# One PSUM bank for the backward chain, a three-bank score ring, and a longer first segment in the backward weave of a mixed-attention kernel

## The chip, the cores and the metric

The kernel runs on one core of a Trainium2 chip. A core has a matrix engine (PE; its weight loads are listed as PEld), a vector engine (DVE), a scalar engine (ACT), GpSimd (POOL) and a queue engine that only issues transfers (SP). Matmuls write to PSUM, a memory of eight banks with 2 KB for each of 128 partitions; DVE and ACT read it from there. Sixteen DMA engines move data for all queues.

The metric is the device time of one launch in microseconds. The kernel before was run three times: 6249.93, 6255.53 and 6257.06 us, median 6255.53 us. The profile is of one more execution, of 6245.49 us, whose span from the first to the last instruction is 6243.7 us. Times of places in the trace are counted from the start of that span.

## The reference

The kernel computes a gated sum of two attention layers on 2048 tokens of width 576, and all gradients. Layer A is multi-query attention with 32 heads of width 18 and one shared key and value. Layer B is a recurrent layer with 32 heads of width 128: it works on 64 segments of 32 tokens, and 8 memory rows go from each segment to the next.

```python
def _A_ref(x, wq, wk, wv, wo):
    q = heads(x @ wq);  k = x @ wk;  v = x @ wv
    p = softmax(einsum('bhqd,bkd->bhqk', q, k) * Dh ** -0.5)
    return merge(einsum('bhqk,bkd->bhqd', p, v)) @ wo

def _B_ref(x, mem0, Wq, Wk, Wv, Wo, seg_len):
    mem = mem0
    for s in range(n_seg):
        h = concatenate([mem, x[:, s * seg_len:(s + 1) * seg_len]], axis=1)
        q, k, v = (einsum('btd,dhe->bhte', h, W) for W in (Wq, Wk, Wv))
        p = softmax(where(mask, einsum('bhqe,bhke->bhqk', q, k) * scale, -1e9))
        o = einsum('bhte,hed->btd', einsum('bhqk,bhke->bhqe', p, v), Wo)
        mem = o[:, :M]
        outs.append(o[:, M:])

out = g * A(x) + (1 - g) * B(x),  g = sigmoid((x * gate_w).sum(-1))
# returned: out and the gradients of all inputs for a given grad_out
```

So the backward pass of layer B is again a recurrence: the gradient of the memory rows goes from segment 63 down to segment 0.

## The kernel before

The program is a row of stages. The one that the change touches is the backward weave, from about 3118 to 4815 us. It puts two unrelated pieces of work together. The **chain** (`b_chain_bwd`) is the backward recurrence of layer B through the 64 segments. The **sweep** (`a_pass2`) is the second pass of layer A's backward attention, which recomputes the scores and gathers the gradients of the shared key and value.

Both are Python generators, and `weave` runs them in turn: one piece of the chain up to its `yield`, then `per_piece` steps of the sweep, which is 1 here. The order is written out by hand (`manual_schedule`), and each engine takes its instructions in the order in which the program issues them. What is left of the sweep runs after the chain.

**A step of the sweep**, n of 0 to 1024, handles two heads of one 128-row query block against 512 keys. It issues: `mm_S(n+1)`, the two score matmuls of the next step into `b_S` (a tile of two banks, one buffer); two matmuls into `b_dP` (one bank each, ring of three); `ex(n+1)`, the exponential of both score banks as one 1024-wide ACT instruction into `b_E`; two DVE multiplications `b_dS = b_dP * b_E` (L1585); and then the sums of step n-1: four matmuls of `b_dS` and `b_E` of that step into the accumulator `b_acc` (one bank). The score and `b_dP` matmuls use 32 rows of the array each, so the four can stand side by side; the four sums use 32 columns each and stand side by side too. Every four steps the SP queue loads one `b_QD` and one `b_SD`, two groups ahead.

**A segment of the chain** has 16 pieces:

- three pieces of `proj_part`: the gradient of the 8 memory rows times `WoT`, 40 matmuls of 512 columns into two banks (`r_pj` and `r_x`), each emptied by ACT into `r_dOm`;
- one of `mem_T` (8 small matmuls; ACT copies to `r_dOT`, DVE makes `r_prod`), one for `pd` (80 small matmuls; DVE makes `r_dS`, POOL spreads it out as `r_dSB`);
- `mem_grad` for three weights (16 small matmuls each into `r_x`, emptied by ACT into `r_dT`), the second and third of them with four `heads` units;
- the rest of the `heads` units, 48 in all: a unit is four matmuls of 288 columns side by side (`r_pj<-WT,r_dT`), 24 units fill one half of the sum, which ACT empties into `r_hs`;
- `sums` in two portions (fp32 matmuls into `r_x`), from which DVE writes the memory gradient `dm` for the next segment.

The eight banks of PSUM are all given out: `r_pj` 1, `r_x` 1, `b_S` 2, `b_dP` 3, `b_acc` 1. The weights `WT` (six transfers of 2304 KB) are loaded on the SP queue by `load_WT`, which the first segment (number 63) calls after its second piece; `WoT` is loaded before the stage, by SP and POOL.

Of the kernel before, what the change touches and what calls it, by code (L numbers as in the profile page):

```python
# [6 lines left out]
ACT = mybir.ActivationFunctionType  # L7
ALU = mybir.AluOpType
AX = mybir.AxisListType
BF16 = mybir.dt.bfloat16  # L10
F32 = mybir.dt.float32
P = 128

D = 576
NKT = 5
# [10 lines left out]
SCALEA = float(DA) ** -0.5  # L26
# [4 lines left out]
class Kern:  # L31
# [178 lines left out]

    def weave(self, chain, sweep, per_piece):
        with self.tc.manual_schedule():
            for _ in chain:
                for _ in range(per_piece):
                    next(sweep, None)
            for _ in sweep:
                pass
# [552 lines left out]
    def gate_load(self, tt, sp):  # L770
        r = slice(tt * P, (tt + 1) * P)
        L = []
        for nm, src, dt in (("o_b", self.b_dram, F32), ("o_go", self.grad_out, BF16)):
            t = sp.tile([P, D], dt, name=nm, bufs=1)
            self.nc.gpsimd.dma_start(t[:], src[r, :])
            L.append(t)
        t = sp.tile([P, NKT, P], BF16, name="o_T", bufs=1)
        self.nc.sync.dma_start_transpose(t[:], self.otok_dram[r, :])
        L.append(t)
        return L  # L780

    def gate(self, tt, L, wo, sp, psum):
        nc = self.nc
        bsb, go, oT = L
        diff = sp.tile([P, D], F32, name="o_diff", bufs=1)
# [23 lines left out]
    def load_WT(self):  # L809
        for wi in (2, 0, 1):  # L810
            for g in range(2):
                self.nc.sync.dma_start(self.WT[wi][:, 16 * g:16 * g + 16, :], self.st_WT[wi][:, 16 * g:16 * g + 16, :])

    def b_chain_bwd(self, keep, sp, psum):
        nc = self.nc
        NSEG = self.NSEG
# [37 lines left out]
        def p_blocks(pT):  # L854
            pq = to_q((pT[:, 1, :],), "p", nc.gpsimd)
            B = sp.tile([P, 8, 4, 8], BF16, name="r_PqB", bufs=1)
            self.expand(B[:], pq[:, 0, :, 0:8], 8)
            return B

        nxt = load(NSEG - 1)  # L860
        PqB = p_blocks(nxt["pT"])
        for s in reversed(range(NSEG)):
            L = nxt
            d_ = dm[s % 2]
            pT = L["pT"]
            nc.gpsimd.dma_start(self.dmT_dram[:, :, s, :], d_[:, :, 0:8])
            dOm = sp.tile([P, 8, E], BF16, name="r_dOm", bufs=1)
            pj = [psum.tile([P, 512], F32, name=nm, bufs=1) for nm in ("r_pj", "r_x")]
            for k, parts in enumerate((((0, (0, 1, 2, 3)),), ((0, (4,)), (1, (0, 1))), ((1, (2, 3, 4)),))):
                for j, kts in parts:  # L870
                    self.proj_part(pj[j], d_, self.WoT, j, kts)
                    if kts[-1] == 4:
                        self.evac(dOm[:, 4 * j:4 * j + 4, :].rearrange("p u e -> p (u e)"), pj[j][:], use="s")
                if s == NSEG - 1 and k == 1:
                    self.load_WT()
                yield
            src = self.mem_T(dOm, psum, "r_x", 1)
            dOT = sp.tile([P, 8, 4, 8], BF16, name="r_dOT", bufs=1)
# [28 lines left out]
            ph = {}  # L907
# [3 lines left out]
            def heads(n):  # L911
                for _ in range(n):
                    wi, hf, u = next(units)
                    if hf not in ph:
                        ph[hf] = psum.tile([P, 288], F32, name="r_pj", bufs=1)
                    for g in range(4):
                        self.mm(ph[hf][32 * g:32 * g + 32, :], lhsT=dT[:, wi, u, :],
                                rhs=self.WT[wi][:, 8 * g + u, 288 * hf:288 * hf + 288],
                                start=(wi == 2 and u == 0), stop=(wi == 1 and u == 7), tp=(0, 32 * g))
                    if wi == 1 and u == 7:  # L920
                        nc.scalar.copy(hs[:, 288 * hf:288 * hf + 288], ph[hf][:])

            def sums(kts):
                for kt in kts:
                    ncols = KT_ROWS[kt]
                    self.mm(pm[0:ncols, kt, :], lhsT=hs[:, kt * P:kt * P + ncols], rhs=self.selF[:, :])
# [13 lines left out]
            mem_grad(0, "r_x", ((rows(L["kx"]), blk(dSB)), (rows(mrow["k"]), blk(dSB, 8))))  # L940
            dSqB = sp.tile([P, 8, 4, 8], BF16, name="r_dSqB", bufs=1)
            self.expand(dSqB[:], dSq[:, 0, :, 0:8], 8)
            heads(4)
            yield
            heads(4)
            mem_grad(1, "r_x", ((rows(mrow["dx"]), [seln] * 8), (rows(mrow["q"]), blk(dSqB))))
            nc.gpsimd.dma_start(self.dTm_dram[s // 16][:, :, s % 16, :], dT[:].rearrange("p w u c -> p w (u c)"))
            if s:
                nxt = load(s - 1)
            yield  # L950
            heads(6)
            yield
            heads(6)
            xq = to_q((pT[:, 0, :], dS[:, 0, :]), "x", nc.gpsimd)
            for c in range(4):
                nc.gpsimd.dma_start(self.pq_dram[s // 4, s % 4, :, c, :, 32 * (s % 4):32 * (s % 4) + 32],
                                    xq[32 * c:32 * c + 8].rearrange("p i u k -> p (i u) k"))
            yield
            heads(4)
            yield  # L960
            heads(6)
            yield
            heads(6)
            pm = psum.tile([P, NKT, 8], F32, name="r_x", bufs=1)
            sums((0, 1))
            yield
            heads(6)
            if s:
# [1 line left out]
            yield  # L970
            heads(6)
            yield
            sums((2, 3, 4))
            dn = dm[1 - s % 2]
            nc.vector.tensor_copy(dn[:, 0:4, 0:8], pm[:, 0:4, :])
            nc.vector.tensor_copy(dn[0:64, 4, 0:8], pm[0:64, 4, :])
            yield
        pt = psum.tile([P, 8, P], BF16, name="r_x", bufs=1)
        for kt in range(NKT):
            rows = KT_ROWS[kt]  # L980
# [412 lines left out]
    def a_qd_end(self, p, qb, pq, absq, sp):  # L1393
        nc = self.nc
        self.mm(pq[0:64, :], lhsT=self.smneg[:, :], rhs=absq[:, :], start=False, stop=True, tp=(0, 0))
        QD = sp.tile([P, 512], BF16, name="a_QDs", bufs=3)
        nc.vector.tensor_copy(QD[:, :], pq[:, :])
        (nc.sync if qb % 2 == 0 else nc.gpsimd).dma_start(self.qd_dram[p][:, qb * 512:(qb + 1) * 512], QD[:, :])

# [131 lines left out]
    def a_pass2(self, keep, sp, psum):  # L1531
        nc = self.nc
        T, NTT = self.T, self.NTT
        KV = keep.tile([P, T], BF16, name="b_KV")
        nc.sync.dma_start(KV[:, :], self.kv_dram[:, :])
        Q, S, E_, D_ = {}, {}, {}, {}
        NC = 4 * NPR * NTT // 4

        def load(c):
            if c < NC:  # L1540
                p, q4 = (c // 4) % NPR, c % 4
                QD = sp.tile([P, 512], BF16, name="b_QD", bufs=3)
                nc.sync.dma_start(QD[:], self.qd_dram[p][:, q4 * 512:(q4 + 1) * 512])
                SD = sp.tile([P, 4, P], BF16, name="b_SD", bufs=3)
                nc.sync.dma_start(SD[:], self.sd_dram[p][:, 4 * q4:4 * q4 + 4, :])
                Q[c] = (QD, SD)

        def pair(n):
            return n // (NPR * NTT), n // 4, n % 4

        def mm_u(dst, n, base):
            kb, c, j = pair(n)
            for i in range(2):
                r = slice(base + 32 * i, base + 32 * i + 32)
                self.mm(dst[i], lhsT=Q[c][0][r, j * P:j * P + P], rhs=KV[r, kb * 512:kb * 512 + 512],
                        tp=(base + 32 * i, 0))

        def mm_S(n):
            S[n] = psum.tile([P, 2, 512], F32, name="b_S", bufs=1)
            mm_u([S[n][:, i, :] for i in range(2)], n, 0)  # L1560

        def ex(n):
            E_[n] = sp.tile([P, 2, 512], BF16, name="b_E", bufs=3)
            nc.scalar.activation(E_[n][:], S.pop(n)[:], ACT.Exp, scale=SCALEA)  # L1564

        load(0)
        load(1)
        mm_S(0)
        ex(0)
        acc = None  # L1570
        NS = NPR * NTT
        NP_ = 4 * NS
        for n in range(NP_ + 1):
            if n < NP_:
                if n % 4 == 2:
                    load(n // 4 + 2)
                if n + 1 < NP_:
                    mm_S(n + 1)
                dP = [psum.tile([P, 512], F32, name="b_dP", bufs=3) for _ in range(2)]
                mm_u([t[:] for t in dP], n, 64)  # L1580
                if n + 1 < NP_:
                    ex(n + 1)
                D_[n] = sp.tile([P, 2, 512], BF16, name="b_dS", bufs=2)
                for i in range(2):
                    nc.vector.tensor_tensor(out=D_[n][:, i, :], in0=dP[i][:], in1=E_[n][:, i, :], op=ALU.mult)  # L1585
            if n > 0:
                o = n - 1
                if o % NS == 0:
                    acc = psum.tile([P, 512], F32, name="b_acc", bufs=1)
                SD = Q[o // 4][1]  # L1590
                src = (D_.pop(o), E_.pop(o))
                for i4 in range(4):
                    self.mm(acc[32 * i4:32 * i4 + 32, :], lhsT=SD[:, o % 4, 32 * i4:32 * i4 + 32],
                            rhs=src[i4 // 2][:, i4 % 2, :],
                            start=(o % NS == 0), stop=(o % NS == NS - 1), tp=(0, 32 * i4))
                if o % NS == NS - 1:
                    dkv = sp.tile([P, 512], BF16, name="b_dkv", bufs=1)
                    nc.scalar.copy(dkv[:], acc[:])
                    k0 = (o // NS) * 512
                    nc.sync.dma_start(self.dkv_dram[:, k0:k0 + 512], dkv[:])  # L1600
            yield
# [229 lines left out]
```

The softmax here doesn't subtract the row's maximum and nothing guards it: scores larger than these inputs give would overflow.

## Time and profile before

| | us | remark |
|---|---|---|
| median of three runs | 6255.5 | 6249.9 to 6257.1 |
| span of the profiled run | 6243.7 | granted PE clock 0.974 in the mean |
| backward weave | 3118 to about 4815 | loads up to 3144, last sums just after 4811 |
| its steady part, segments 62 to 0 | 3196 to 4807 | PE busy 1484.9, DVE 1403.6, ACT 1207.6, POOL 577.3 of 1611 us |
| its first part | 3118 to 3196 | DMA busy nearly all of it up to 3181 |

In a group line the parts are: line, engine, operation, what is written and read, the shape, the count, then busy time and mean nanoseconds of one, then the idle time of the engine just ahead of these instructions and what ended it. Matmuls that stand side by side overlap, so a group's busy time is less than count times mean. All matmuls have line 66 because a helper records them; they are told apart by the tiles that they write and read. Consecutive instructions of ACT or DVE overlap a little in their records, since the next one starts while the last one is still writing.

### The profile page before, as it was taken

To read this page: it belongs to the slowest core of one execution; us is meant where nothing else is said; L and a number is where in the kernel's file an instruction comes from. 1 tells how busy PE (TensorE), PEld (TensorE's weight loads), DVE (VectorE), ACT (ScalarE), POOL (GpSimd) and SP (SyncE) were. 2 spreads that over 40 slices of the span, in tenths; PEclk is the share of its full clock that TensorE was granted. 3 is DMA by queue.
4 is the path that set the end of the run, shared out by engine and by line. 5 is a ranking of instruction groups with operands and counts; after the bars stand their busy time and mean duration, and the time that the engine had idled before them with its cause. 6 is when DMAs were issued, how large, how long until landed. Compare 5 with 4: busy or idle time off the path is not lost.

```text
span 6243.7 us, 208736 instructions
## 1 busy us (share of the span) xinstructions
PE 5691.9 (91%) x88611; PEld 3321.0 (53%) x88822; DVE 3743.0 (60%) x7061; ACT 3500.1 (56%) x5105; POOL 1952.9 (31%) x3451
## 2 busy tenths in 40 slices
PE   7898999999999985999869999999998999899996
PEld 5443444444444434777735555555554777674443
DVE  4336777777777773666558888888887111121111
ACT  3326787778777873656557777777776222111101
POOL 3002343434343342444423333333333111122213
PEclk9999999999999997999989999999999999999998
DMA  4646666666675536999864444444444999996643
GB/s 153 223 151 120 126 125 127 126 127 125 127 125 107 105 85 181 249 257 258 245 207 107 109 109 108 108 111 109 110 108 103 244 244 250 243 261 196 222 150 114
DMA packets 1368111, 991.97 MB, mean 159 GB/s; under 512 B 931613, under 2 KB 1184806, under 8 KB 1356486
## 3 DMA queue, kind: packets, MB, share of 16 engines
q1 hardware_dynamic: 1285030, 780.53, 52.1%
q0 software_dynamic: 82144, 198.05, 10.0%
q8 instruction: 696, 11.40, 0.8%
q14 instruction: 241, 1.97, 0.1%
HBM read 552.41 MB, written 384.76 MB: 150 GB/s over the span
## 4 chain that ended last, share of the span: by engine, by line
PE 64%; ACT 15%; issue 9%; DMA 6%; SPq 3%; POOL 2%; DVE 1%; ACTq 0%; POOLq 0%; DVEq 0%
ACT b_E L1564 10%; PE w_acc L66 10%; PE a_acc L66 8%; PE c_x L66 6%; PE b_S L66 6%; PE a_S L66 5%; PE c_pj L66 5%; PE p_pb L66 4%; PE r_pj L66 4%; ACT a_E L1422 3%; PE r_x L66 2%; DMA dsx_dram<-x_dS 2%; PE x_tr L71 2%; PE b_acc L66 2%; PE x_po L66 1%
## 5 line engine op out<-in xcount | busy, mean ns | idle before, releaser
L1455 DVE TENSOR_TENSOR a_W<-a_dP,a_E 128x512 bf16<-128x512 f32 x2048 | 1316.2, 685 | 413.2 <-PE a_dP L66 289.7
L1585 DVE TENSOR_TENSOR b_dS<-b_dP,b_E 128x512 bf16<-128x512 f32 x2048 | 1312.9, 683 | 241.8 <-issue 119.6
L1564 ACT ACTIVATE b_E<-b_S 128x1024 bf16<-128x1024 f32 x1024 | 1048.9, 1024 | 446.3 <-PE b_dP L66 322.0
L1422 ACT ACTIVATE a_E<-a_S 128x1024 bf16<-128x1024 f32 x1024 | 1050.6, 1026 | 218.5 <-PE a_dP L66 182.9
L66 PE MATMUL b_S<-b_KV,b_QD 32*128 32x512 bf16 x2048 | 401.1, 382 | 155.2 <-ACT b_E L1564 100.7
L66 PE MATMUL r_pj<-WT,r_dT 128*32 128x288 bf16 x12288 | 493.5, 287 | 1.5 <-issue 1.5
L66 PE MATMUL w_acc<-w_d,w_h 128*128 128x512 bf16 (+1 forms) x2352 | 471.0, 379 | 2.5
L66 PE MATMUL a_acc<-a_E,l_VK 128*32 128x512 bf16 x4096 | 401.6, 380 | 27.9 <-ACT a_acs L1460 27.8
L66 PE MATMUL a_S<-a_QD,l_KV 32*128 32x512 bf16 x2048 | 398.5, 384 | 24.7 <-ACT a_E L1422 15.3
L66 PE MATMUL b_acc<-b_dS,b_SD 128*32 128x512 bf16 x2048 | 419.3, 391 | 0.6 <-DVE b_dS L1585 0.2
L66 PE MATMUL a_acc<-a_W,l_WK 128*32 128x512 bf16 x4096 | 411.8, 390 | 0.2 <-DVE a_W L1455 0.2
L66 PE MATMUL b_acc<-b_E,b_SD 128*32 128x512 bf16 x2048 | 404.0, 391 | 0.0
L66 PE MATMUL b_dP<-b_KV,b_QD 32*128 32x512 bf16 x2048 | 401.2, 386 | 0.0
L66 PE MATMUL a_dP<-a_QD,l_KV 32*128 32x512 bf16 x2048 | 398.1, 385 | 0.0
L66 PEld LDWEIGHTS <-r_dT 128*32 128x32 bf16 x12288 | 333.2, 97 | 80.5 <-issue 2.6
L1055 DVE COPY y_T<-y_pt 128x512 bf16<-128x512 bf16 x256 | 97.1, 420 | 461.5 <-PE y_pt L71 461.4
L66 PEld LDWEIGHTS <-b_QD 32*128 32x128 bf16 x4096 | 164.9, 91 | 345.7 <-issue 284.7
L66 PEld LDWEIGHTS <-w_h 128*128 128x128 bf16 (+1 forms) x2400 | 213.0, 100 | 244.6 <-issue 3.4
L66 PEld LDWEIGHTS <-hm 128*32 128x32 bf16 x7680 | 188.2, 96 | 186.4 <-issue 14.6
L1041 ACT CAST y_tdk<-y_pk 128x512 bf16<-128x512 f32 x128 | 75.1, 587 | 377.0 <-PE y_pk L66 212.5
L66 PEld LDWEIGHTS <-l_KV 32*128 32x128 bf16 x4096 | 118.9, 91 | 297.4 <-issue 275.3
L66 PE MATMUL y_pdx<-WT,y_T 128*128 128x288 bf16 x2048 | 272.8, 287 | 0.0
(416 smaller groups left out, 11401.9 us busy)
## 6 DMA issues: line engine op xcount, KB each, us to landing
b_QD<-qd_dram SPq DMA_DIRECT2D x256, 128.0 KB
b_SD<-sd_dram SPq DMA_DIRECT2D x256, 128.0 KB
dOx_dram<-p_tok SPq DMA_DIRECT2D x16, 1024.0 KB
c_vx<-vx_dram SPq DMA_DIRECT2D x256, 64.0 KB
krow_dram<-c_k POOLq DMA_DIRECT2D x64, 256.0 KB, 3.0
qrow_dram<-c_q POOLq DMA_DIRECT2D x64, 256.0 KB, 3.4
vrow_dram<-c_v POOLq DMA_DIRECT2D x64, 256.0 KB, 3.0
x_q<-qx_dram SPq DMA_DIRECT2D x32, 512.0 KB
```

Of the source, the lines that this page charges most:

```text
L66: return self.nc.tensor.matmul(out, lhsT, rhs, start=start, stop=stop, tile_position=tp, skip_group_check=True)
L71: return self.nc.tensor.transpose(out, in_, self.identB[b:b + nrows, b:b + nrows], tile_position=tp)
L1041: nc.scalar.copy(d[w][:, r, :], pk[:])
L1055: nc.vector.tensor_copy(T_[t][w][:], pt[:])
L1422: nc.scalar.activation(E_[n][:], S.pop(n)[:], ACT.Exp, scale=SCALEA)
L1455: nc.vector.tensor_tensor(out=W_[n][:, i, :], in0=dP[i][:], in1=E_[n][:, i, :], op=ALU.mult)
L1564: nc.scalar.activation(E_[n][:], S.pop(n)[:], ACT.Exp, scale=SCALEA)
L1585: nc.vector.tensor_tensor(out=D_[n][:, i, :], in0=dP[i][:], in1=E_[n][:, i, :], op=ALU.mult)
```

## The change

All of it lies in the backward weave.

- **Weave.** A piece may now yield a number; then so many sweep steps follow it (a plain `yield` still means one).
- **Chain on one bank.** `r_pj` is gone; the projection, the `heads` sums and everything else use `r_x`. The projection has two pieces of 20 matmuls instead of three. The third `mem_grad` and the second one stand alone, all `heads` come after them in eight pieces of six units, and `sums` is one piece at the end. There are 16 pieces still; the last yields `s % 2`, so in even segments no sweep step stands between `sums` and the next segment's projection.
- **First segment.** `load_WT` moves ahead of the loop and to the POOL queue, behind a one-column copy `r_seen` that reads the last block of `WoT`. Then 11 sweep steps follow ahead of the first projection, 4 after the third `mem_grad`, and 10 after each of the first two `heads` pieces.
- **Sweep.** `b_S` is a ring of three one-bank tiles (two for each step), so the exponential is two 512-wide instructions. The sums of step n-2, not n-1, are issued in step n; `b_E` has four buffers and `b_dS` three. `b_dkv` shares the ring of `b_QD`.

```diff
-            for _ in chain:
-                for _ in range(per_piece):
+            for steps in chain:
+                for _ in range(per_piece if steps is None else steps):
...
-                self.nc.sync.dma_start(self.WT[wi][:, 16 * g:16 * g + 16, :], self.st_WT[wi][:, 16 * g:16 * g + 16, :])
+                self.nc.gpsimd.dma_start(self.WT[wi][:, 16 * g:16 * g + 16, :], self.st_WT[wi][:, 16 * g:16 * g + 16, :])
...
+        seen = sp.tile([P, 1], BF16, name="r_seen", bufs=1)
+        nc.gpsimd.tensor_copy(seen[:], self.WoT[:, NKT - 1, 0:1])
+        self.load_WT()
+        yield 11
         for s in reversed(range(NSEG)):
+            first = s == NSEG - 1
...
-            pj = [psum.tile([P, 512], F32, name=nm, bufs=1) for nm in ("r_pj", "r_x")]
-            for k, parts in enumerate((((0, (0, 1, 2, 3)),), ((0, (4,)), (1, (0, 1))), ((1, (2, 3, 4)),))):
-                for j, kts in parts:
-                    self.proj_part(pj[j], d_, self.WoT, j, kts)
-                    if kts[-1] == 4:
-                        self.evac(dOm[:, 4 * j:4 * j + 4, :].rearrange("p u e -> p (u e)"), pj[j][:], use="s")
-                if s == NSEG - 1 and k == 1:
-                    self.load_WT()
+            for j in range(2):
+                pj = self.proj_mem(d_, self.WoT, j, psum, "r_x", 1)
+                self.evac(dOm[:, 4 * j:4 * j + 4, :].rearrange("p u e -> p (u e)"), pj[:], use="s")
                 yield
...
-                        ph[hf] = psum.tile([P, 288], F32, name="r_pj", bufs=1)
+                        ph[hf] = psum.tile([P, 288], F32, name="r_x", bufs=1)
...
-            heads(4)
-            yield
-            heads(4)
+            yield
             mem_grad(1, "r_x", ((rows(mrow["dx"]), [seln] * 8), (rows(mrow["q"]), blk(dSqB))))
...
-            yield
+            yield 4 if first else 1
             heads(6)
-            yield
+            yield 10 if first else 1
+            heads(6)
+            yield 10 if first else 1
             heads(6)
...
-            pm = psum.tile([P, NKT, 8], F32, name="r_x", bufs=1)
-            sums((0, 1))
...
-            sums((2, 3, 4))
+            pm = psum.tile([P, NKT, 8], F32, name="r_x", bufs=1)
+            sums(range(NKT))
...
-            yield
+            yield s % 2
...
-            S[n] = psum.tile([P, 2, 512], F32, name="b_S", bufs=1)
-            mm_u([S[n][:, i, :] for i in range(2)], n, 0)
+            S[n] = [psum.tile([P, 512], F32, name="b_S", bufs=3) for _ in range(2)]
+            mm_u([t[:] for t in S[n]], n, 0)
...
-            E_[n] = sp.tile([P, 2, 512], BF16, name="b_E", bufs=3)
-            nc.scalar.activation(E_[n][:], S.pop(n)[:], ACT.Exp, scale=SCALEA)
+            E_[n] = sp.tile([P, 2, 512], BF16, name="b_E", bufs=4)
+            for i, t in enumerate(S.pop(n)):
+                nc.scalar.activation(E_[n][:, i, :], t[:], ACT.Exp, scale=SCALEA)
...
-        for n in range(NP_ + 1):
+        for n in range(NP_ + 2):
...
-                D_[n] = sp.tile([P, 2, 512], BF16, name="b_dS", bufs=2)
+                D_[n] = sp.tile([P, 2, 512], BF16, name="b_dS", bufs=3)
...
-            if n > 0:
-                o = n - 1
+            if n > 1:
+                o = n - 2
...
-                    dkv = sp.tile([P, 512], BF16, name="b_dkv", bufs=1)
+                    dkv = sp.tile([P, 512], BF16, name="b_dkv", tag="b_QD", bufs=3)
```

More of the change, by code (lines that the diff above doesn't have):

```diff
@@ L958, in b_chain_bwd @@
             yield
-            heads(4)
+            heads(6)
             yield
@@ L1541, in load @@
                 p, q4 = (c // 4) % NPR, c % 4
-                QD = sp.tile([P, 512], BF16, name="b_QD", bufs=3)
+                QD = sp.tile([P, 512], BF16, name="b_QD", tag="b_QD", bufs=3)
                 nc.sync.dma_start(QD[:], self.qd_dram[p][:, q4 * 512:(q4 + 1) * 512])
```

## The prediction

> **What bounds the kernel now.** I read the page first for the place of the stage, then the chain of waits inside one segment, then the timelines of PE and DVE there, and last the stretches at its start.
>
> The chain of waits, from 3954 us on (start, length, what):
>
> ```profile
> 3961.01 1.03 ACT b_E L1564
> 3962.08 0.39 PE b_S L66 x2
> 3962.47 0.08 PE b_dP L66 x2
> 3962.56 1.03 ACT b_E L1564
> 3963.63 0.39 PE b_S L66 x2
> 3964.11 1.03 ACT b_E L1564
> 3965.18 0.39 PE b_S L66 x2
> ```
>
> A closed circle: the scores need the bank that the exponential reads, the exponential needs the scores. 3962.08 to 3963.63 to 3965.18 is 1.55 us each time. That is the floor of a step while PE, DVE and ACT each have less to do.
>
> The PE timeline shows where a step is longer:
>
> ```profile
> 3958.59 0.39 PE L66 MATMUL b_S<-b_KV,b_QD 32*128 32x512 bf16 x2
> 3958.92 0.39 PE L66 MATMUL b_acc<-b_dS,b_SD 128*32 128x512 bf16 x2
> ...
> 3959.14 0.91 PE L66 MATMUL r_pj<-WT,r_dT 128*32 128x288 bf16 x24
> 3959.99 0.61 PE L66 MATMUL r_x<-selF,r_hs 128*128 128x8 f32 x4
> 3960.53 0.39 PE L66 MATMUL b_S<-b_KV,b_QD 32*128 32x512 bf16 x2
> ...
> 3974.82 0.39 PE L66 MATMUL b_acc<-b_dS,b_SD 128*32 128x512 bf16 x2
> ...
> 3975.15 0.19 PE L66 MATMUL r_x<-r_dSB,r_kx 128*128 128x32 bf16 x1
> ...
> 3975.65 0.67 PE L66 MATMUL r_pj<-WT,r_dT 128*32 128x288 bf16 x16
> 3976.25 0.39 PE L66 MATMUL b_S<-b_KV,b_QD 32*128 32x512 bf16 x2
> ```
>
> From start to start: scores and dP 0.33, sums 0.22, six heads units 0.85, two of the five portions of `sums` 0.54; a `mem_grad` 0.50 after 0.33 for the sums and the change of tile shape. One segment is 12 steps at 1.55, and 1.94 (heads with `sums`), 1.76 and 1.65 (`mem_grad` with heads) and 1.61 (a step behind `r_xq` on DVE): 25.56 us. The `dmT_dram` transfers of two segments start at 3196.46 and 3222.01, 25.55 us apart. 63 segments: 3196 to 4807, 25.57 us each.
>
> DVE, same place, and then the stretches (length, busy PE, PEld, DVE, ACT, POOL, clock, DMA share, GB/s):
>
> ```profile
> 3956.23 2.56 DVE L1585 TENSOR_TENSOR b_dS<-b_dP,b_E 128x512 bf16<-128x512 f32 x4
> ...
> 3961.05 1.29 DVE L1585 TENSOR_TENSOR b_dS<-b_dP,b_E 128x512 bf16<-128x512 f32 x2 [0.65 <-issue]
> ```
>
> ```profile
> 3144.00:3162.00 18.00, 14.09 (x239) 5.78 (x239) 9.84 (x18) 10.05 (x14) 3.83 (x6) 0.69 1.02 422
> 3162.00:3181.00 19.00, 0.26 (x4) 0.11 (x4) 0.00 (x0) 0.36 (x1) 1.20 (x3) 0.50 1.06 407
> ...
> 3196.00:4807.00 1611.00, 1484.87 (x31327) 833.59 (x31323) 1403.63 (x2511) 1207.63 (x1510) 577.30 (x1006) 1.00 0.43 108
> ```
>
> Four `b_dS` of 0.68 in 2.56 give a pitch of (2.56 - 0.68) / 3 = 0.627, so 1.25 us of DVE a step. DVE is busy 22.3 us a segment (1403.6 / 63), PE 23.6. The circle hides how near they are. From 3162 to 3181 nothing computes: a `b_QD` stands behind `WT` in the SP queue.
>
> **What the Trainium skill says.** PSUM — Partial Sum Buffer, PSUM bank collisions: engines must not touch one bank and quadrant at once, so writers wait for readers by bank. The trace agrees: scores restart 0.05 after the exponential ends. ScalarE: Activation LUTs, What ACT_TABLE_LOAD costs: an activation takes 186 ns + 0.833 ns an element, and neighbours overlap by 93 ns. The trace has 1024 ns for 1024 (1039 by the page) and 579 to 588 for the 512-wide copies of `r_dOm`. TensorEngine Tiling (Array Packing), Key Properties: changing the tiling mode drains the array; the 0.33 above against 0.22 agrees. DMA: Bandwidth & Descriptors, Queues, rings and completion order: an engine goes round its queues packet by packet. No run here shows how that falls out between `WT` and the sweep's loads.
>
> **The change part by part**, against the profiled span, which stands 12 us under the median.
>
> *Score ring.* The circle goes: the next step's second score matmul needs only the first half of the exponential, about 0.48 + 0.6 after the step's start, so 1.13. Two 512-wide exponentials cost ACT 2 x 0.5 for 0.92, +0.1 a step, beside PE (by the page's price 2 x 0.52). ACT then has some 15.5 x 1.0 + 3 in a segment of over 24. The next floor is DVE: the second `b_dP` of a step takes the bank of the first `b_dS` of the last step, which starts 0.52 after the scores and lasts 0.68: 1.20 at best, 1.25 when DVE is never idle.
>
> *Sums two steps late.* Same matmuls; the wait of PE for `b_dS` (0.2 in the 1.61 step) goes. Buffers are SBUF only. One more iteration is under 1 us. `b_dkv` in the `b_QD` ring delays one load at four places; the loads run two groups ahead: nothing.
>
> *A segment now*, step with piece:
> - Projection, two pieces: 0.55 + 1.19 each. (12 and 16 matmuls show 0.82 and 1.04, so 20 give 1.26, and the next scores start about 0.07 before that end.) The second waits for its bank: ACT empties the first 0.59 after its end, PE is back after 0.55 less a tail: +0.15. Sum 3.63.
> - `mem_T`, `pd`, three `mem_grad`: PE has 0.98 + 1.50 + 3 x 1.19 = 6.1, but DVE 5 x 1.25 + `r_prod` 0.22 + `r_dS` 0.22 + `r_dspad` and `r_dsq` 0.58 (start to start in the DVE timeline) = 7.3, and it waits in order for `r_dOT`, 0.1: 7.4.
> - Eight pieces of six heads: 8 x (0.33 + 0.22 + 0.84) = 11.1; `r_xq` (0.63) overruns by 0.3, `r_pq` and two handovers of the bank 0.1: 11.5.
> - `sums`: 0.55 + 0.11 + 10 x 0.13 = 1.96. In even segments the step is gone, but PE waits about 0.5 for `dm` (3965.11 to 3965.65 before): no gain.
>
> Together 24.5, against 25.57: 1.07 less, x 63 = -67 us. It has 15.5 steps, not 16; the other half steps are paid at the start.
>
> *First segment.* It now holds 48 sweep steps: 24.5 + 32.5 x 1.25 + 3 for the clock of 0.69 = 68 us from the first scores, for 52 (3144.5 to 3196.3): +17 if no load is late. `WT` on POOL frees the SP queue of 4.0 us of issues, but its 14 MB still take 39 us (3141.6 to 3180.7). If its 18 KB rows alternate with the 1 KB rows of `b_QD` and `b_SD`, the sweep gets only 8 to 12 steps in by 3180 and ends the segment near 3231: +35. `r_seen` waits for `WoT`, but PE and `r_ppad` ahead of it wait as long (3136, 3137.4); behind it stand `WT` and the chain's stores, which nobody needs soon. I take +26.
>
> Net -67 + 26 = -41: 6255.5 - 41 = **6214 us** (span about 6203).
>
> **The rivals.**
> 1. *One bank turns into the circle* (slower). Eight handovers of `r_x` a segment, each a copy of 0.37 to 0.59 plus whatever exponential half ACT is in. Before, two banks and 1.55 us steps hid this. For it: ACT is in order, and in the 1.25 us steps it still holds exponentials at the next piece. Against: a step's 0.55 to 0.66 of PE stands between pieces. At 0.2 us more each: 26.1 a segment, +33 + 26: 6314. It decides from 25.2 on, 0.09 us a handover.
> 2. *PE and DVE overlap better* than stretch by stretch. The sums above without the waits and with 15.5 steps give PE 22.3 in all, DVE 15.5 x 1.25 + 2.4 = 21.8. At 23.5: 63 x 2.07 = -130, +22: 6147. For it: rings one step deeper. Against: the `b_dP` ring is still three.
> 3. *A wash*: `WT` starves the sweep (+35) and small waits bring 25.0: -36 + 35: 6255. The change then doesn't fill the gap as it says.
>
> **How the numbers follow.** Forecast 0.52, its own range 6189 to 6243 (24.2 to 24.9 a segment, start +20 to +30); rival 2 0.18; rival 3 0.12; rival 1 0.18. About 0.2% (12.5 us) can be told from no change: faster 0.52 + 0.18, same 0.12, slower 0.18. The range leaves out the fastest end of rival 2 (about 0.07) and the larger part of rival 1 (about 0.12): 6158 to 6288.
>
> **What would show it.** Score matmuls that no longer wait for `b_E`; `dmT_dram` transfers about 49 us apart for two segments; heads steps of 1.39; DVE without gaps from `mem_T` to the third `mem_grad`; PE idle before `dOm` and `r_x` under 0.2. The start is judged by when segment 62 begins (3213 to 3231) and by waits for `b_QD`. I am wrong in the main step if the segments come 25.2 us apart or more, or if PE waits for ACT at most handovers.

## The result, and the profile after

| | before | after |
|---|---|---|
| median of six runs each, us | 6254.82 (6248.08 to 6262.6) | 6217.08 (6210.39 to 6222.2) |
| span of the profiled run, us | 6243.7 | 6215.3 |
| first segment: issue of the `WoT` loads to the start of segment 62, us | 76.4 (3120.03 to 3196.46) | 119.2 (3123.86 to 3243.09) |
| mean from start to start of segments 62 to 0 (62 intervals), us | 25.68 | 24.34 |

The ratio is 0.994 (95% interval 0.9927 to 0.9953): 37.7 us less by the medians, where 41 less was forecast. The two parts of the forecast sum are each further off than that. The 62 intervals between segment starts bring 62 x (24.34 - 25.68) = -83 us, and the first segment takes +42.8. Together that is -40 for the stage. A mark behind the stage says the same: its first transfer of `h_hist` starts 35.9 us earlier than before (4832.03 for 4867.92), although the stage began 3.8 us later in this profile, so 39.7 were gained in it. The two spans differ by only 28.4, because this execution of after took 3.8 us more ahead of the stage and 7.5 us more behind that mark.

Segment starts are read from the POOL timeline, where one `dmT_dram` transfer leaves for each segment. Columns: start, length, engine, line, operation, count, and in brackets the idle time ahead and what ended it. First the kernel after:

```profile
3123.86 1.18 POOL L516 DMA_DIRECT2D WoT<-st_WoT  x2 [11.95 <-DMA dqx_dram<-x_dq]
...
3243.09 0.89 POOL L871 DMA_DIRECT2D dmT_dram<-dm  x1 [2.34 <-DVE dm L975]
3267.32 0.90 POOL L871 DMA_DIRECT2D dmT_dram<-dm  x1 [2.35 <-DVE dm L975]
3291.42 0.89 POOL L871 DMA_DIRECT2D dmT_dram<-dm  x1 [2.34 <-DVE dm L975]
...
4752.28 0.90 POOL L871 DMA_DIRECT2D dmT_dram<-dm  x1 [2.34 <-DVE dm L975]
```

The same view of the kernel before, its last segment:

```profile
4788.46 0.90 POOL L866 DMA_DIRECT2D dmT_dram<-dm  x1 [2.73 <-DVE dm L976]
```

(4752.28 - 3243.09) / 62 is 24.34; most intervals are 24.23 and 24.10 in turn, so two segments take 48.3, as the forecast asked for (about 49). The starts of before, 3196.46 to 4788.46, give 1592.0 / 62 = 25.68. The forecast had used 25.57, from 1611 us over 63 segments; most intervals of before are 25.57, but every few segments one takes 0.3 to 1.0 more.

The PE timeline of after inside one segment, the score and `b_dP` matmuls and one piece of heads:

```profile
3980.09 0.39 PE L66 MATMUL b_S<-b_KV,b_QD 32*128 32x512 bf16 x2
...
3980.70 0.37 PE L66 MATMUL b_dP<-b_KV,b_QD 32*128 32x512 bf16 x1 [0.22 <-DVE b_dS L1585]
...
3981.83 0.39 PE L66 MATMUL b_S<-b_KV,b_QD 32*128 32x512 bf16 x2
...
3982.42 0.91 PE L66 MATMUL r_x<-WT,r_dT 128*32 128x288 bf16 x24
3983.26 0.39 PE L66 MATMUL b_S<-b_KV,b_QD 32*128 32x512 bf16 x2
...
3984.66 0.39 PE L66 MATMUL b_S<-b_KV,b_QD 32*128 32x512 bf16 x2
...
3986.05 0.39 PE L66 MATMUL b_S<-b_KV,b_QD 32*128 32x512 bf16 x2
...
3993.97 1.27 PE L66 MATMUL r_x<-selF,r_hs 128*128 128x8 f32 x10
...
3995.59 1.26 PE L66 MATMUL r_x<-WoT,dm 128*32 128x512 bf16 x20 [0.35 <-DVE dm L975]
3996.78 0.39 PE L66 MATMUL b_S<-b_KV,b_QD 32*128 32x512 bf16 x2
```

PE's waits above 0.15 us in after, from 3250 to 4700 (what waited and what released it; us in all, times, longest); two more are of 0.2 us each:

```profile
PE b_dP L66 <- DVE b_dS L1585: 13.4, 60, 0.3
PE r_x L66 <- DVE dm L975: 10.4, 30, 0.3
PE b_S L66 <- DMA b_QD<-qd_dram: 5.7, 8, 2.2
```

No score is among these with a wait for the exponential. A step with heads takes 3984.66 - 3983.26 = 1.40 and then 1.39. The `mem_grad` step from 3980.09 to 3981.83 is longer, 1.74, and what ends the wait in it is DVE: the second `b_dP` matmul of the step waits for a bank that `b_dS` still reads. The last three lines of the timeline are an even segment, with no step between `sums` and the projection: PE is idle for 0.35 until DVE has written `dm`.

The DVE timeline at the same place:

```profile
3973.11 1.29 DVE L1585 TENSOR_TENSOR b_dS<-b_dP,b_E 128x512 bf16<-128x512 f32 x2 [0.43 <-issue]
3975.43 1.29 DVE L1585 TENSOR_TENSOR b_dS<-b_dP,b_E 128x512 bf16<-128x512 f32 x2 [1.03 <-ACT r_dOm L63]
...
3980.00 6.51 DVE L1585 TENSOR_TENSOR b_dS<-b_dP,b_E 128x512 bf16<-128x512 f32 x10
```

DVE has gaps around the projection (0.43 and 1.03 here) and none from `mem_T` to the third `mem_grad`: PE sets the pace in one stretch, DVE in the other.

In the groups of after (line, engine, operation, what is written and read, shape, count, busy time and mean ns, idle time ahead and its releaser) the single biggest wait of the score matmuls is now a transfer:

```profile
L1564 ACT ACTIVATE b_E<-b_S 128x512 bf16<-128x512 f32 x2048 | 1114.7, 599 | 253.9 <-PE b_dP L66 210.6
...
L66 PE MATMUL b_S<-b_KV,b_QD 32*128 32x512 bf16 x2048 | 417.7, 389 | 57.9 <-DMA b_QD<-qd_dram 57.3
```

51.5 of those 57.3 us (41.78, 5.26 and 4.43) are in the first segment. (The 41.78 count from the end of PE's work in the stage before; 23.4 of them pass ahead of the issue of `WT`. Before has 26.6 us of waits for `b_QD` there and 18.4 for `WoT`.) The PE timeline of this segment and the stretches there (length, busy PE, PEld, DVE, ACT, POOL, clock, DMA share, GB/s), both of after:

```profile
3161.61 1.01 PE L66 MATMUL b_S<-b_KV,b_QD 32*128 32x512 bf16 x3 [41.78 <-DMA b_QD<-qd_dram]
...
3173.32 0.60 PE L66 MATMUL b_S<-b_KV,b_QD 32*128 32x512 bf16 x2 [5.26 <-DMA b_QD<-qd_dram]
...
3184.61 0.61 PE L66 MATMUL b_S<-b_KV,b_QD 32*128 32x512 bf16 x2 [4.43 <-DMA b_QD<-qd_dram]
```

```profile
3144.00:3162.00 18.00, 0.39 (x3) 0.16 (x4) 0.00 (x0) 0.00 (x0) 3.30 (x6) 0.50 1.02 388
3162.00:3190.00 28.00, 15.15 (x86) 2.98 (x86) 13.27 (x22) 12.56 (x24) 0.00 (x0) 0.50 0.83 338
```

The DMA engines are full from 3144 to 3162 and PE, DVE and ACT do nothing: the first scores come 18.4 us after `WT` began to be issued (3143.22), and the scores of only eight steps are begun before 3184.61. The 32 extra steps (11, 3, 9 and 9 above one step a piece) were to fill the time in which `WT` arrives, and for much of that time their own inputs are not there. Before has begun just as many, eight, when its wait for `b_QD` ends at 3180.74: the gap holds no more steps than it did.

### The profile page after: what moved, and what is told of

Same layout as the page of the kernel before. It is cut to its first block, busy times and chain, and to the rows that moved or that the text cites. A ratio compares the mean times of both kernels' runs of the same rounds, so it can differ in the third digit from the quotient of the medians.

```text
span 6215.3 us, 210597 instructions
## 1 busy us (share of the span) xinstructions
PE 5734.9 (92%) x88611; PEld 3278.1 (53%) x88822; DVE 3724.6 (60%) x7061; ACT 3545.8 (57%) x6129; POOL 1950.7 (31%) x3458
## 5 line engine op out<-in xcount | busy, mean ns | idle before, releaser
L1585 DVE TENSOR_TENSOR b_dS<-b_dP,b_E 128x512 bf16<-128x512 f32 x2048 | 1292.8, 680 | 203.0 <-issue 90.1
L1564 ACT ACTIVATE b_E<-b_S 128x512 bf16<-128x512 f32 x2048 | 1114.7, 599 | 253.9 <-PE b_dP L66 210.6
L66 PE MATMUL b_dP<-b_KV,b_QD 32*128 32x512 bf16 x2048 | 471.5, 386 | 16.1 <-DVE b_dS L1585 15.4
L66 PE MATMUL b_S<-b_KV,b_QD 32*128 32x512 bf16 x2048 | 417.7, 389 | 57.9 <-DMA b_QD<-qd_dram 57.3
L66 PE MATMUL r_x<-WT,r_dT 128*32 128x288 bf16 x12288 | 467.5, 287 | 0.0
L66 PE MATMUL a_S<-a_QD,l_KV 32*128 32x512 bf16 x2048 | 398.9, 384 | 25.9 <-ACT a_E L1421 15.5
L66 PE MATMUL b_acc<-b_dS,b_SD 128*32 128x512 bf16 x2048 | 406.4, 394 | 3.3 <-DMA b_SD<-sd_dram 2.8
L66 PEld LDWEIGHTS <-b_SD 128*32 128x32 bf16 x4096 | 105.3, 93 | 324.2 <-issue 306.7
```

The costliest lines, as they stand in the source:

```text
L66: return self.nc.tensor.matmul(out, lhsT, rhs, start=start, stop=stop, tile_position=tp, skip_group_check=True)
L1564: nc.scalar.activation(E_[n][:, i, :], t[:], ACT.Exp, scale=SCALEA)
```

## The experiments

Each experiment is compared with runs of the kernel before that were made beside it, as a ratio, because the median of before moved between 6247 and 6259 us from one set of runs to the next. In the same terms after has 0.994. The diffs are against the kernel after.

### The score ring alone: `e3_old_ring`

The one-bank chain, the late sums and the moved steps stay; the scores go back to one tile of two banks with one 1024-wide exponential.

```diff
-            S[n] = [psum.tile([P, 512], F32, name="b_S", bufs=3) for _ in range(2)]
+            S[n] = psum.tile([P, 2, 512], F32, name="b_S", bufs=1)
...
-            for i, t in enumerate(S.pop(n)):
-                nc.scalar.activation(E_[n][:, i, :], t[:], ACT.Exp, scale=SCALEA)
+            nc.scalar.activation(E_[n][:], S.pop(n)[:], ACT.Exp, scale=SCALEA)
```

> The changed kernel with the scores as before: b_S one tile of two banks, one buffer, and one exponential of 1024; the one-bank chain, the late sums and the moved steps stay. Theory A (the circle of scores and exponential was the floor of a step): no step under 1.55 us again; a segment takes about 25.9 us for 24.3, 63 x 1.6 = +100, and 32 bare steps cost 0.3 more each, +10: about 6325, slower than the kernel before. Theory B (the gain is from the late sums and the new order of the chain): within 20 us of 6217.

Measured: 6320.39 us (6318.86 to 6330.52), before 6251.53, ratio 1.0113 (1.0098 to 1.0128). PE timeline of this kernel:

```profile
3980.66 0.39 PE L66 MATMUL b_S<-b_KV,b_QD 32*128 32x512 bf16 x2 [0.57 <-ACT b_E L1563]
3982.21 0.39 PE L66 MATMUL b_S<-b_KV,b_QD 32*128 32x512 bf16 x2
3983.76 0.39 PE L66 MATMUL b_S<-b_KV,b_QD 32*128 32x512 bf16 x2 [0.32 <-ACT b_E L1563]
3985.31 0.39 PE L66 MATMUL b_S<-b_KV,b_QD 32*128 32x512 bf16 x2 [0.33 <-ACT b_E L1563]
```

The circle of 1.55 us is back, and it swallows the heads pieces that need less. Segments come 25.83 and 25.71 us apart, and the extra steps of the first segment are paid on top, so the kernel is slower than before. Theory A holds. The ring is worth 1.7% of the time (1.0113 against 0.994): without it the other parts of the change gain nothing. The bank that the chain gives up is what pays for it.

### The sums two steps late: `e4_sums_one_late`

```diff
-        for n in range(NP_ + 2):
+        for n in range(NP_ + 1):
...
-            if n > 1:
-                o = n - 2
+            if n > 0:
+                o = n - 1
```

> The changed kernel with the sums of step n-1, not n-2, in step n; ring of three and all else kept. Theory A (a step then has to wait for the second b_dS of the step before, which ends 0.52 + 1.31 = 1.83 us after that step's scores, so a heads step needs 1.83 + 0.22 + 0.84 - 1.39 - 0.05 = about 1.45 for 1.39 and a step behind DVE work of the chain more): 0.5 to 1.5 us a segment, +30 to +95: 6250 to 6310. Theory B (the extra step of delay isn't needed once the ring is there): within 10 us of 6217.

Measured: 6266.61 us (6264.56 to 6270.33), before 6251.53, ratio 1.0026 (1.0015 to 1.0037). PE timeline of this kernel, one step of heads:

```profile
3983.25 0.39 PE L66 MATMUL b_S<-b_KV,b_QD 32*128 32x512 bf16 x2
...
3983.57 0.52 PE L66 MATMUL b_acc<-b_dS,b_SD 128*32 128x512 bf16 x2
3983.72 0.39 PE L66 MATMUL b_acc<-b_E,b_SD 128*32 128x512 bf16 x2
3983.80 1.05 PE L66 MATMUL r_x<-WT,r_dT 128*32 128x288 bf16 x24
3984.78 0.39 PE L66 MATMUL b_S<-b_KV,b_QD 32*128 32x512 bf16 x2
```

The pair of sums that reads `b_dS` stands for 0.52 us where it otherwise takes 0.39, since the second `b_dS` is not written yet (the DVE timeline has four `b_dS` in 2.71 us from 3982.37, so the second ends at about 3983.7); all that is behind it on PE waits too, and the step takes 1.53 for 1.39 in after. Segments are 25.26 and 25.14 apart. The later sums are worth 0.86% once the ring is there (1.0026 against 0.994), as theory A had it. With the 1.55 us circle in place they had nothing to win (0.2 in one step of before); with the circle gone they are needed.

### Which engine sets which stretch: `e5_dve_mid` and `e6_dve_proj`

Both add one more DVE transpose for each segment, whose result nobody reads. It shows 0.69 us in the records, and a neighbour starts a little before it ends. In the first it stands in the second `mem_grad` piece, in the stretch that was put down to DVE; in the second behind the first projection, in a stretch put down to PE.

```diff
+        def more_dve():
+            pad = pads["x"]
+            o = sp.tile([P, 2, 8, 32], BF16, name="r_xq", bufs=1)
+            nc.vector.transpose(o[:].rearrange("p i u k -> p (i u k)"), pad[:].rearrange("p i u k -> p (i u k)"))
...
# e5_dve_mid, in mem_grad's second piece
+            more_dve()
# e6_dve_proj, in the projection
+                if j == 0:
+                    more_dve()
```

> The changed kernel with one more DVE transpose of r_xpad (0.63 us from start to start, its result unused) in every segment, behind the second mem_grad, where the step-by-step working has DVE as the bound. Theory A (a segment is the sum of stretches, each with its own bound): +0.6 us a segment, 64 x 0.6 = +38: 6255. Theory B (PE sets the whole segment, DVE has about 2 us to spare in it): no change, 6217.

> The same extra DVE transpose, but behind the first projection piece, where DVE stands idle for 0.4 and 1.0 us between its pairs. Theory A (stretches with their own bounds): no more than 0.1 us a segment, 6217 to 6223. Theory C (the sum of DVE work bounds the segment): +0.6 us a segment wherever it stands: 6255.

Measured: 6249.8 us (6241.41 to 6264.03), ratio 1.0007 (0.9998 to 1.0015), for the first, and 6204.86 us (6202.68 to 6207.56), ratio 0.9936 (0.9921 to 0.9951), for the second; before 6247.29. The same instruction costs 0.67% in one place (1.0007 - 0.994, some 42 us) and nothing that can be seen in the other. Segments come 25.03 us apart in the first, in the mean, and 24.35 in the second, against 24.34. PE's waits from 3250 to 4700 us, first `e5_dve_mid`, then `e6_dve_proj`:

```profile
PE b_dP L66 <- DVE b_dS L1591: 28.0, 116, 0.3
```

```profile
PE b_dP L66 <- DVE b_dS L1592: 12.9, 59, 0.2
```

After has 13.4 us in 60 such waits. In `e5_dve_mid` the first heads step, in which PE waits for DVE to catch up, takes 2.02 us for the 1.43 of after in most segments; that is 0.59 of the 0.69 that a segment is longer. The rest is uneven: this profile has nine stretches of 3.4 us between 3250 and 4775 in which the granted PE clock was 0.5 (after has one), and what brings them on no run shows. Theory A holds for both places: DVE is the bound in the `mem_grad` stretch and has room to spare around the projection.

### What delays the start: `e1_small_rows`

`WT` comes in 24 transfers of 4 heads each (576 KB, rows of 4.5 KB for each partition) instead of six (2304 KB, rows of 18 KB). The bytes are the same.

```diff
-            for g in range(2):
-                self.nc.gpsimd.dma_start(self.WT[wi][:, 16 * g:16 * g + 16, :], self.st_WT[wi][:, 16 * g:16 * g + 16, :])
+            for g in range(8):
+                self.nc.gpsimd.dma_start(self.WT[wi][:, 4 * g:4 * g + 4, :], self.st_WT[wi][:, 4 * g:4 * g + 4, :])
```

> The changed kernel with one edit: WT is loaded in 24 transfers of 4 heads (rows of 4.6 KB) instead of 6 of 16 heads (rows of 18.4 KB), same queue, same bytes. Theory A (the sweep's first loads take turns with WT row by row, so each 1 KB row of KV, QD or SD waits for an 18 KB row): with rows a quarter as long the first score matmul, at 3161.6 us now, 18 us after KV is issued, starts about 12 us earlier, waits for b_QD in the first segment fall from about 51 us to under 20, and the time falls by 15 to 25 us, to about 6195. Theory B (the first part is bound by the bytes of WT and WoT alone): the same time within 5 us, 6217.

Measured: 6199.18 us (6196.04 to 6215.48), before 6251.53, ratio 0.9921 (0.9905 to 0.9937). The interval overlaps that of after, so the total does not settle it; the trace does. The PE timeline of this kernel and, below it, its POOL timeline:

```profile
3151.80 1.01 PE L66 MATMUL b_S<-b_KV,b_QD 32*128 32x512 bf16 x3 [32.47 <-DMA b_SD<-sd_dram]
...
3187.11 0.19 PE L66 MATMUL r_x<-r_dSB,r_kx 128*128 128x32 bf16 x1 [10.33 <-POOL r_dSB L205]
```

```profile
3141.95 4.26 POOL L812 DMA_DIRECT2D WT<-st_WT  x8
3149.58 0.53 POOL L812 DMA_DIRECT2D WT<-st_WT  x1 [3.37 <-DMA WT<-st_WT]
...
3178.06 0.85 POOL L871 DMA_DIRECT2D dmT_dram<-dm  x1 [0.90 <-DMA WT<-st_WT]
...
3185.97 1.08 POOL L205 TENSOR_TENSOR r_dSB<-r_dS,bmask 128x512 bf16<-128x512 bf16 x1
```

The first scores come 9.9 us after the first `WT` issue, not 18.4, and the later waits of the scores for `b_QD` are gone. The edit makes rows and transfers shorter at once; the DMA packets tell the two apart. In after, from 3156 to 3159 us (queue and kind, packets, MB, share of the 16 engines):

```profile
q0 software_dynamic: 65, 1.20, 92.9%
q1 hardware_dynamic: 67, 0.07, 6.4%
```

The first is the queue of `WT`, with 18 KB to a packet, the second that of the sweep's loads, with 1 KB (rows of `b_QD` and `b_SD`; `b_KV`, loaded ahead of them, has rows of 4 KB, not 1 KB as the expectation says): a packet is a row here, and the two queues take turns one for one (22 and 22, 21 and 22, 22 and 23 in the three microseconds). In `e1_small_rows` they are again even, 243 and 245 packets from 3152 to 3155, with rows of 4.5 KB. So what starved the sweep was the length of the rows with which its own loads take turns. The Trainium skill (DMA: Bandwidth & Descriptors, Queues, rings and completion order) says that an engine goes round its queues and drains a packet before it switches, and the counts agree with that.

Segment 62 starts only 9 us earlier all the same (110.3 us after the `WoT` loads for 119.2), where theory A would have the whole time fall by about 22. A new wait takes part of it: POOL issues no more than eight `WT` transfers before it waits for earlier ones, so the last goes out at 3176.62. The chain's own POOL work, `dmT_dram`, four `dOm_dram` and then `r_dSB`, stands behind and waits for landings too, and PE waits 10.33 us for `r_dSB`. This profile is of the slowest of the four runs, 6215.48 us; the others took 6196.0 to 6201.2.

### The moved steps: `e2_no_shift`, `e8_qd_early`, `e9b_qd_noshift`

`e2_no_shift` gives every piece one step, so that nothing is moved to the first segment and 16 steps go with every segment. The steps that move back are 32, one for each even segment; the expectation counts 31.

```diff
-        yield 11
+        yield 0
...
-            yield 4 if first else 1
+            yield
...
-            yield 10 if first else 1
+            yield
...
-            yield s % 2
+            yield
```

> The changed kernel with every chain piece followed by one sweep step again: no 11, 4, 10 and 10 in the first segment, and a step after sums in even segments too; 1024 steps stand in the chain, none is moved. Theory A (in even segments PE waits about 0.35 us for dm where the step was, so leaving out 31 steps there saved only about 0.15 us each, while a bare step in the first segment costs 1.2 to 1.25): the first segment is about 40 us shorter, the 32 even segments about 0.15 us longer each (+5), together about -35 us: 6182. Theory B (the extra steps fill time in which PE would wait for WT anyway): no gain, 6217, or slower.

Measured: 6219.65 us (6211.24 to 6224.46), before 6251.53, ratio 0.9947 (0.9932 to 0.9962): no gain over after, as theory B had said, but for another reason than B's. The first segment does what A said: 77.9 us from the `WoT` loads to segment 62 (3120.89 to 3198.80), 41 less than after. The other segments give it back: (4758.51 - 3198.80) / 62 = 25.16. PE's waits in this kernel from 3250 to 4700, then the SP queue around 3994, where the columns are those of a timeline:

```profile
PE b_S L66 <- DMA b_QD<-qd_dram: 40.0, 44, 4.2
```

```profile
3990.77 0.43 SPq L829 DMA_DIRECT2D r_vmT<-vmT_dram  x1
...
3998.91 0.89 SPq L843 DMA_DIRECT2D r_q<-qrow_dram  x1
3999.84 0.44 SPq L1542 DMA_DIRECT2D b_QD<-qd_dram  x1
```

After has 5.7 us in 8 such waits. The first line is the first of the chain's loads, the last the `b_QD` load behind them. The sweep's loads come every four steps. With 16 steps a segment they keep one place in it, and it is right behind the 14 loads with which the chain fetches its next segment: 9.1 us of SP issues (3990.77 to 3999.84). With 15.5 steps the place drifts through the segment. So the odd half step also kept the loads from one bad place, which neither theory had.

`e8_qd_early` keeps the moved steps and issues the load of `b_QD` two steps earlier; `e9b_qd_noshift` has that and the diff of `e2_no_shift`.

```diff
-        load(0)
-        load(1)
+        for c in range(2):
+            load_q(c)
+            load_s(c)
...
+                if n % 4 == 0:
+                    load_q(n // 4 + 2)
...
-                    load(n // 4 + 2)
+                    load_s(n // 4 + 2)
...
-                    dkv = sp.tile([P, 512], BF16, name="b_dkv", tag="b_QD", bufs=3)
+                    dkv = sp.tile([P, 512], BF16, name="b_dkv", tag="b_SD", bufs=3)
```

> The changed kernel with one edit: the load of b_QD is issued two steps earlier than that of b_SD; the steps stay moved to the first segment. Which half of the gain of the version with both edits (ratio 0.986) belongs to which? Theory A: the moved steps cost it, and the earlier load only repairs what 16 steps a segment would break. With 15.5 steps the steady part waits for b_QD only 5.7 us in all, so the early load alone gains at most that: ratio 0.993 to 0.994, segment 62 still about 115 to 120 us behind the start of the WoT loads, 24.25 to 24.34 us a segment. Rival B: the earlier load is the gain by itself, since it also gets b_QD in ahead of WT at the start: ratio 0.986 to 0.988, segment 62 some 85 to 90 us behind the WoT loads.

> No step moved (every piece followed by one step, as in e2_no_shift), and b_QD issued two steps earlier in the program, ahead of the chain's loads of a segment and not behind them; b_dkv shares the ring of b_SD instead. Theory A (in e2_no_shift the 40 us won in the first segment were lost again because 16 steps a segment put each fourth b_QD load right behind the chain's 14 loads on SP, 44 waits): the waits for b_QD in the steady part fall under 5 us, a segment takes 24.4 us and not 25.2, and the time is about 6180. Theory B (16 steps a segment are slower for another reason): still 25.2 a segment, about 6220.

| | ratio to before | `WoT` loads to segment 62, us | mean segment, us |
|---|---|---|---|
| after | 0.994 (0.9927 to 0.9953) | 119.2 | 24.34 |
| `e2_no_shift` | 0.9947 (0.9932 to 0.9962) | 77.9 | 25.16 |
| `e8_qd_early` | 0.9922 (0.9906 to 0.9939) | 115.2 | 24.24 |
| `e9b_qd_noshift` | 0.9864 (0.9848 to 0.988) | 76.2 | 24.27 |

In microseconds: `e8_qd_early` 6209.28 (6202.39 to 6212.44), before 6259.41; `e9b_qd_noshift` 6160.25 (6152.21 to 6167.8), before 6247.29. Theory A holds for both: alone, the earlier load brings little (0.9922, an interval that overlaps that of after), and with it the waits for `b_QD` in a kernel of 16 steps a segment are gone (0.2 us from 3250 to 4700). Without moved steps and with it, the kernel is 1.36% faster than before and faster than after. The POOL timeline of `e9b_qd_noshift`:

```profile
3117.11 1.18 POOL L516 DMA_DIRECT2D WoT<-st_WoT  x2 [11.96 <-DMA dqx_dram<-x_dq]
...
3193.31 0.89 POOL L871 DMA_DIRECT2D dmT_dram<-dm  x1 [2.35 <-DVE dm L975]
3217.53 0.90 POOL L871 DMA_DIRECT2D dmT_dram<-dm  x1 [2.35 <-DVE dm L975]
...
4698.33 0.89 POOL L871 DMA_DIRECT2D dmT_dram<-dm  x1 [2.35 <-DVE dm L975]
```

Its segments have 16 steps and take 24.22 each in most cases; those of after, with 15.5 steps, take 24.23 and 24.10 in turn. A step that is left out in an even segment therefore saves 0.13 us. The wait table of `e9b_qd_noshift` says why: PE's 30 waits for `dm` (10.4 us from 3250 to 4700 in after) do not occur in it, since the step stands where PE would wait. In the first segment a moved step costs about nine times that: from `e9b_qd_noshift` to `e8_qd_early` it grows by 39.0 us for 32 steps, 1.22 each.

### All three together: `e9_all_three`

`e9b_qd_noshift` with the short rows of `e1_small_rows`.

> e9b_qd_noshift and also WT in 24 transfers with rows of 4.6 KB. Theory A: the first scores come about 9 us earlier as in e1_small_rows, but the heads of the first segment wait for WT, which needs its 33 to 39 us of transfer either way; so only about -5 against e9b_qd_noshift: 6175. If the first segment is not bound by WT: -9, 6171.

Measured: 6160.95 us (6153.21 to 6162.32), before 6247.29, ratio 0.9862 (0.9845 to 0.9879): the same as without the short rows. Neither forecast gain came. The first scores come early (3142.9, 9.4 us after `WT` begins), but segment 62 starts 80.2 us after the `WoT` loads, against 76.2. The PE timeline has the wait for POOL again, longer than in `e1_small_rows`:

```profile
3176.73 0.18 PE L66 MATMUL r_x<-r_dSB,r_kx 128*128 128x32 bf16 x1 [24.67 <-POOL r_dSB L205]
```

So this run does not show what an earlier sweep alone would be worth without the moved steps: the wait behind POOL's `WT` issues comes with it.

## Why the prediction was right, and where it was not

The direction, the size and the reasons for the shorter segment held: 6217 us for a forecast of 6214. Inside it, two terms are off by about the same amount with opposite signs, -83 for -67 and +42.8 for +26. That the total lies within 3 us of the forecast is therefore luck. The segments lie in the range that was given for them (24.2 to 24.9); the start does not (+20 to +30), and segment 62 begins at 3243.1 (3239.3 without the 3.8 us by which this stage began later), not between 3213 and 3231.

- **Score ring.** Right. The circle goes (after), and comes back at 1.55 us with the old tile (`e3_old_ring`).
- **Sums two steps late.** Right that the wait for `b_dS` goes. Its worth was only put at 0.2 in one step of before; once the circle is gone, sums one step late cost 0.86% (`e4_sums_one_late`).
- **A segment now.** 24.5 was forecast, 24.34 came. By stretches in the segment from 3970.82, forecast and measured: projections 3.63 and 3.69; `mem_T` to the third `mem_grad` 7.4 and 7.32; heads 11.5 and 11.47; `sums` 1.96 and 1.87 (the last from the segment before, 3968.95 to 3970.82). The floors behind these were named rightly: a transpose more for DVE is paid in the second stretch and not in the first (`e5_dve_mid`, `e6_dve_proj`).
- **The segment before.** 25.57 was the usual segment, not the mean; from start to start it is 25.68. Together with the previous point the gain is 1.34 a segment and not 1.07: -83 us for 62 intervals, where -67 was forecast for 63.
- **First segment.** This is the mis-sized term: +26 taken, +42.8 measured. Its working was +17 if no load is late (its 68 for 52 give 16), and I had added 9 for late loads. Measured from the first scores, after needs 81.5 us to segment 62. Of these 12.5 are waits for `b_QD` and `b_SD` (1.21, 5.26, 1.56 and 4.43), so 69.0 without them, where 68 was worked out; before needs 52.0, so +17.0. What was missing is that the first scores themselves come late: 37.7 us after the `WoT` loads, for 24.5 before, +13.3. The forecast let the sweep start at once and starve later, but `WT` is issued just ahead of `b_KV` and the first `b_QD`, and they take turns with its rows as well. 17.0 + 13.3 + 12.5 = 42.8. That short rows bring the first scores 9 us forward, and that the packets alternate, shows why the loads are late (`e1_small_rows`). The lateness costs so much only together with the moved steps: in `e2_no_shift` the first scores come as late, 37.5 us after the `WoT` loads, and the first segment takes 77.9 us, close to the 76.4 of before. From there to after it grows by 41.3 us for 32 steps, 1.29 each, the price of steps that fall into no gap.
- **In even segments "no gain".** Right (0.13 us), and more telling than I made of it. If the step saves nothing where it is left out and is paid in full at the start, then moving it is a loss by the forecast's own figures, +26 for nothing. The text booked it as part of the price of the change and did not draw the conclusion; `e9b_qd_noshift` did, and is 0.76% faster than after (0.58% faster than `e8_qd_early`, which has the same earlier load and the moved steps).
- **Rivals.** Rival 1, one bank as a new circle, did not come: the segments come 24.34 us apart, where 25.2 was to decide for it. PE's list of waits from 3250 to 4700 has none of `r_x` for ACT, which empties it at the handovers, and heads pieces, with a handover every fourth, mostly come every 1.39 us. The list leaves out waits up to 0.15 us, so small ones may be there. Rival 2 did not come either, since DVE holds the `mem_grad` stretch. Rival 3 had the right mechanism for the start, `WT` starving the sweep, and its +35 was nearer than my +26; the small waits that were to bring 25.0 a segment were not there.

Left open: how far a different order of `WT` and the sweep's first loads could repair the start with the steps still moved. With short rows the wait behind POOL's `WT` issues takes the place of the starved loads, and an order that avoids both was not tried, with the moved steps or without.

## What to carry to other kernels

Price a software pipeline stretch by stretch, each with its own floor, because removing one circle uncovers a different engine in each; an extra instruction in one stretch at a time shows which engine that is. Work that is moved into an idle gap pays only if its own inputs can arrive in that gap, and if its absence saves something where it was; look first at what the engine would wait for there. When a periodic load runs beside a periodic burst on one queue, work out which place in the burst it falls on before changing either period.

## What the runs showed that was not expected

- Six transfers with 18 KB rows hold the first scores back until 18.4 us after their issue, 24 transfers with 4.5 KB rows and the same bytes until 9.9 us.
- POOL had at most eight of the 24 `WT` transfers under way and then waited for earlier ones; the next POOL instructions of the chain waited with it, and PE waited 10.33 us for them in one kernel and 24.67 us in the other.
- With 16 steps a segment instead of 15.5 a load every four steps falls behind the same 9.1 us of SP issues each time, which costs 0.9 us a segment: 25.16, and 24.27 in the kernel with 16 steps that issues the load two steps earlier.
- Rows of 18 KB and rows of 1 KB from two queues passed one for one, 65 and 67 in 3 us, so that the short ones had 6.4% of the DMA time.
